# A linear-attention recurrence with two MLPs on one core: fewer, wider TensorE instructions and a later output part

## The chip, the cores and the metric

One core of a Trainium2 chip. The engines are TensorE (PE, with its weight loads PEld), VectorE (DVE), ScalarE (ACT), GpSimd (POOL) and SyncE (SP, which issues the DMAs). The metric is the device time of one execution in microseconds (us).

## The reference

A recurrence over 768 time steps for 4 x 8 heads with a 40 x 40 state each, then two MLPs over the 3072 x 320 result.

```python
for t in range(S):
    y[:, :, t] = np.einsum('bhd,bhde->bhe', rt, state)
    Sa = np.einsum('bhde,bhe->bhd', state, at)
    state = state * wt[:, :, None, :] - np.einsum('bhd,bhe->bhde', Sa, bt) + np.einsum('bhd,bhe->bhde', vt, kt)
h = x @ w_in;  solu = h * softmax(h);  x = layernorm(solu) * g_ln @ w_out    # first MLP, 320 -> 1024 -> 320
h = x @ w_in2; x = (max(h, 0) + alpha * min(h, 0)) @ w_out2                # second MLP, 320 -> 2048 -> 320
```

The weights arrive as 64-bit floats and are decoded to fp32 on the chip.

## The kernel before, in words

The 768 steps are 12 windows of 64 steps, each of two chunks of 32: 24 chunks, g = 0 to 23. The 32 heads lie in two halves e (partitions 0 to 63 and 64 to 127), each as 2 x 8 (pe, p). Within a chunk the recurrence is written as matrix products.

One call of slot (L1108) records chunk g. Its stages in order: load_g (L577) issues the loads of the next chunk's v (VUS, time-major; VUF, feature-major) and r (YS). stage_x (L591) multiplies a by state and v into px, copied to XP. stage_u (L607) multiplies by the chunk's inverse NT into pu, copied to VUS as U. stage_uf (L630) makes U again, feature-major, in pf, copied to VUF. stage_i (L645) puts the state into the bank pst with an identity matmul, stage_st (L658) adds the products of k and b with v and U there, and ACT copies the new state to the other VUS buffer. stage_g2 (L696) makes the masked products of r with k and U (pg, then DVE times mask into YS). stage_s (L681) brings the new state to the layout of KBS (pss). stage_y (L718) makes the output py, which DVE scales to Yt and ACT and DVE split into high and low parts Y. After an odd chunk x_move (L748) stores Y to DRAM (xd) and loads it back as xt, the first MLP's input.

Between these stages side (called at the points a to z of a slot) records gen1 (L454, chunk products of a with k and b), trans (L556, kbf transposed into KBS) and the two matmul parts of the inverse for four chunks (units, L526), whose other steps run on DVE.

The first MLP is cut into tasks (mlp_tasks, L1058): in slot g the queue gets mm1 of token tile g - 3 (16 matmuls h), the transposes tr1 and the 8 matmuls mm2 (po, with weights wo) of tile g - 4, and tr2 (ptx). They stand in one queue, in order, and are put where the recurrence would wait.

PE, ACT, DVE and POOL have their order written out by a planner that runs while the program is built: now[0] is its clock, note (L239) adds a duration, run books the other engines, until (L308) goes on when a value is due and pops tasks (pop, L273) or, where none is ready, zero or busy matmuls; pace (L293) notes a group of matmuls and fills in where too few array columns were counted lately. The transfers' order on SP is left to the framework. bank gives one of 4 PSUM banks. On the chip each engine takes its own list in order and waits for semaphores.

The first four slots have no MLP tasks but the last of them; their fillers are busy matmuls (L326), later ones zero (L286). The last four token tiles of the first MLP run after the slots, interleaved with the second MLP (phase2).

Of the kernel before, what the change touches and what calls it, by code (L numbers as in the profile page):

```python
# [27 lines left out]
KQ, RES = 8, 10  # L28
# [16 lines left out]
def tile_kernel(ctx: ExitStack, tc: tile.TileContext, w_fm, a0_fm, a_fm, kb_fm, r_fm, v_fm, v_tm,  # L45
# [117 lines left out]
    queue, now, seen = [], [0.0], []  # L163
# [333 lines left out]
    def inverse(W):  # L497
# [28 lines left out]
        def units(p, lhsT, rhs, rows, ls):  # L526
            for l in ls:
# [28 lines left out]
    def trans(w, q):  # L556
# [49 lines left out]
    def stage_u(g):  # L606
# [4 lines left out]
        for p in range(8):  # L611
# [12 lines left out]
    def blank(p):  # L624
# [3 lines left out]
        note(0.11 * p.shape[1] / 8, 8 * p.shape[1])  # L628

    def stage_uf(g, pe):  # L630
        NT, l0 = st["NT", g // 4], (g % 4) * 8
        vuf = VUF[g % 2]
        pf, bk = bank([128, 8, 32], "pf")
        blank(pf)
        for p in range(8):
            for e, o in EO:
                q = 2 * e + pe
                r = slice(q * 32, q * 32 + 32)
                nc.tensor.matmul(pf[o:o + 40, p, :], lhsT=XP[r, p * D:p * D + D], rhs=NT[r, l0 + p, :],  # L639
                                 start=True, stop=True)  # L640
            pace(0.08, 32)
        t = run("A", 0.38, lambda: nc.scalar.copy(out=vuf[:, pe * 8:pe * 8 + 8, 1, :], in_=pf[0:104]), now[0] + PL)
# [996 lines left out]
```

## Time and profile before

| | us |
|---|---|
| median of 3 timed runs (lowest, highest) | 1143.43 (1137.14, 1145.4) |
| the profiled execution: its own time | 1150.15 |
| its span, first to last instruction | 1148.4 |
| PE busy in the span | 1049.8 |
| the slots | about 72 to 747 |

Up to 38 us the first windows are prepared. The first chunk's stage_x runs there; it then waits for the first inverse. From 72 us on the slots follow one another until the last py at 746 us; then come the rest of the first MLP and the second, where PE is busy nearly throughout.

### The profile page before, as it was taken

The page shows a single profiled execution, that of the slowest core. Times are in us where ns is not written, and L with a number is a line of the kernel's source. Part 1 is how long each engine was busy: PE and PEld are TensorE (multiplying, and loading weights), DVE is VectorE, ACT ScalarE, POOL GpSimd, SP SyncE. Part 2 cuts the span into 40 slices and gives each one's busy share as a digit, 9 for nine tenths or more (in the row PEclk, how much of TensorE's full clock was granted, in tenths as well). Part 3 has the DMA queues.
Part 4 walks back from the last instruction along what each step waited for, and adds up shares of the span by engine and source line. Part 5 has one row for each costly group of instructions (what it writes and reads, how often), then busy time and mean ns, then how long its engine had stood idle before and what let it go on. Part 6 is the DMA issues. An engine that isn't in the chain of part 4 may idle for free.

```text
span 1148.4 us, 42660 instructions
## 1 busy us (share of the span) xinstructions
PE 1049.8 (91%) x19078; PEld 818.5 (71%) x19078; DVE 615.7 (54%) x1150; ACT 553.0 (48%) x1269; POOL 298.6 (26%) x352
## 2 busy tenths in 40 slices
PE   6689788889989998989898899989999999999997
PEld 2456566566667666756676667778899999999997
DVE  8838576657587745864765132354444444444333
ACT  1446437565678556844755466668512121212121
POOL 7401020112221321132201110234333333333333
PEclk9689788899999898988998899999999999999998
DMA  6613334352545353433634232246302020201010
GB/s 172 183 47 100 96 85 119 107 152 57 155 127 140 93 151 86 106 93 94 173 82 128 80 93 63 70 158 187 126 1 69 1 69 1 69 1 46 1 24 14
DMA packets 103169, 103.95 MB, mean 91 GB/s; under 512 B 37828, under 2 KB 80580, under 8 KB 102980
## 3 DMA queue, kind: packets, MB, share of 16 engines
q1 hardware_dynamic: 102980, 101.16, 31.9%
q8 instruction: 151, 2.47, 0.9%
q14 instruction: 38, 0.31, 0.1%
HBM read 75.71 MB, written 25.43 MB: 88 GB/s over the span
## 4 chain that ended last, share of the span: by engine, by line
PE 75%; DMA 7%; issue 5%; ACT 5%; DVE 3%; POOL 1%; SPq 1%; POOLq 0%; DVEq 0%; ACTq 0%
PE ph L1274 15%; PE po L841 9%; PE h L771 7%; PE acc L1292 5%; PE acc L1293 5%; PE acc L1294 5%; PE pf L639 3%; PE pss L687 3%; PE py L728 3%; PE zero L286 2%; PE pst L667 2%; PE busy L326 2%; DMA raw<-in_w_in_dram 2%; PE pst L654 2%; PE pg L706 2%
## 5 line engine op out<-in xcount | busy, mean ns | idle before, releaser
L1281 POOL TENSOR_TENSOR gll<-gt,gh 128x512 fp32r<-128x512 f32 (+1 forms) x112 | 128.1, 1144 | 227.9 <-ACT gh L1280 226.9
L806 DVE TENSOR_SCALAR gt<-ph,al 128x512 f32<-128x512 f32 (+1 forms) x112 | 75.5, 675 | 201.7 <-PE ph L1274 201.5
L1280 ACT CAST gh<-gt 128x512 fp32r<-128x512 f32 (+1 forms) x112 | 62.4, 558 | 250.3 <-DVE gt L807 213.4
L841 PE MATMUL po<-wo,ln 128*128 128x320 f32 x384 | 133.1, 484 | 2.4 <-ACT ln L833 1.7
L841 PEld LDWEIGHTS po<-wo,ln 128*128 128x128 f32 x384 | 74.5, 207 | 30.6 <-issue 7.1
L771 PE MATMUL h<-w1h,xt 128*128 128x512 f32 x240 | 95.9, 455 | 0.0
L1292 PE MATMUL acc<-w2h,gh 128*128 128x320 f32 x288 | 88.8, 308 | 0.0
L1293 PE MATMUL acc<-w2l,gh 128*128 128x320 f32 x288 | 88.8, 308 | 0.0
L1294 PE MATMUL acc<-w2h,gll 128*128 128x320 f32 x288 | 88.7, 308 | 0.0
L583 POOL MEMSET YS<- 64x512 f32 x44 | 23.1, 524 | 228.7 <-PE py L728 227.5
L902 POOL TENSOR_TENSOR raw<-em 128x512 f32<-128x512 f32 (+1 forms) x28 | 42.6, 1527 | 122.4 <-DVE em L893 77.7
L713 DVE TENSOR_TENSOR YS<-pg,mask 64x256 f32<-64x256 f32 x96 | 40.5, 422 | 57.1 <-PE pg L706 55.5
L807 DVE SCALAR_TENSOR_TENSOR gt<-ph,gt 128x512 f32<-128x512 f32 (+1 forms) x112 | 68.8, 615 | 3.8
L771 PE MATMUL h<-w1l,xt 128*128 128x512 f32 x144 | 66.9, 465 | 0.6 <-issue 0.6
L1274 PE MATMUL ph<-w1h,w2h 128*128 128x512 f32 x180 | 59.3, 394 | 0.0
L786 POOL TENSOR_TENSOR sm<-sm,const 128x1 f32<-128x1 f32 x24 | 14.2, 590 | 165.0 <-ACT sm L783 165.0
L567 ACT COPY KBS<-pt 64x160 f32<-64x160 f32 x192 | 55.1, 287 | 3.1 <-PE pt L563 0.5
L1293 PEld LDWEIGHTS acc<-w2l,gh 128*128 128x128 f32 x288 | 54.1, 188 | 1.4
L1292 PEld LDWEIGHTS acc<-w2h,gh 128*128 128x128 f32 x288 | 54.1, 188 | 1.3
L1294 PEld LDWEIGHTS acc<-w2h,gll 128*128 128x128 f32 x288 | 54.1, 188 | 0.0
L771 PEld LDWEIGHTS h<-w1h,xt 128*128 128x128 f32 x240 | 47.9, 209 | 8.5
L881 DVE TENSOR_SCALAR em<-raw 128x512 int32<-128x512 int32 (+1 forms) x39 | 17.8, 456 | 67.1 <-DMA raw<-in_w_in_dram 46.2
(186 smaller groups left out, 2407.3 us busy)
## 6 DMA issues: line engine op xcount, KB each, us to landing
kbf<-in_kb_fm_dram SPq DMA_DIRECT2D x24, 416.0 KB
x2d<-x SPq DMA_DIRECT2D x24, 320.0 KB
raw<-in_w_in_dram SPq DMA_DIRECT2D x14, 512.0 KB
raw<-in_w_out_dram SPq DMA_DIRECT2D x13, 512.0 KB
xd<-Y SPq DMA_DIRECT2D x24, 256.0 KB
xt<-xd SPq DMA_DIRECT2D x12, 512.0 KB
wt<-in_w_fm_dram SPq DMA_DIRECT2D x24, 211.7 KB
VUS<-in_v_tm_dram SPq DMA_DIRECT2D x48, 80.0 KB
```

Source lines behind the costliest of these rows:

```text
L567: t = run("A", 0.29, lambda k=k, c=c, r=r, o=o: nc.scalar.copy(out=k[r:r + 64, 1 - r // 64, q * 4:q * 4 + 4, :], in_=pt[64 * c:64 * c + 64 ...
L771: nc.tensor.matmul(st["h"][:, ns], lhsT=l, rhs=r, start=j == 0, stop=j == len(ops) - 1)
L806: nc.vector.tensor_scalar(out=tmp, in0=h, scalar1=0.0, scalar2=al, op0=ALU.min, op1=ALU.mult)
L807: nc.vector.scalar_tensor_tensor(out=o, in0=h, scalar=0.0, in1=tmp, op0=ALU.max, op1=ALU.add)
L841: nc.tensor.matmul(po, lhsT=st["ln", t][:, piece], rhs=wo1[:, piece], start=piece == 0, stop=piece == K1 - 1)
L902: (nc.vector if eng == "V" else nc.gpsimd).tensor_tensor(out=o, in0=f32(m), in1=f32(e), op=ALU.mult)
L1274: nc.tensor.matmul(p, lhsT=l, rhs=r, start=j == 0, stop=j == len(ops) - 1)
L1280: nc.scalar.copy(out=gh, in_=t)
L1281: nc.gpsimd.tensor_tensor(out=gll, in0=t, in1=f32(gh), op=ALU.subtract)
L1292: nc.tensor.matmul(acc, lhsT=gh[:, cs], rhs=oh, start=f == 0, stop=False)
L1293: nc.tensor.matmul(acc, lhsT=gh[:, cs], rhs=ol, start=False, stop=False)
L1294: nc.tensor.matmul(acc, lhsT=gll[:, cs], rhs=oh, start=False, stop=f == K2 - 1)
```

## The change

It has seven parts. (1) gen1 and stage_g2 use one weight tile of 64 columns where they used two of 32. (2) stage_uf makes U feature-major with transposes of VUS rows, 16 to a bank of its own for each half e, in place of products of XP with NT. (3) stage_i is gone: stage_st starts its own bank, and DVE adds the old state while it writes the new one. (4) stage_s uses transposes, with a bank for each half. (5) uf, g2 and y of chunk g - 1 stand in slot g, the load of r and feature-major v after that y; the last slot holds the parts of both chunks. (6) the planner's note counts PE instructions into pages of 128 and lets its clock wait for a page; pace may pop tasks ahead of such a wait. (7) the points of trans move.

```diff
+PAGE, FETCH, RATE = 128, 3.7, 0.03
...
-KQ, RES = 8, 10
+KQ, RES, SPARE = 8, 10, 6
...
-    def note(dt, n):
+    def note(dt, n, r=0):
+        page[0] += r
+        if page[0] >= PAGE and not plain():
+            page[0] -= PAGE
+            t, page[1] = page[1] + FETCH, max(now[0], page[1] + FETCH)
+            while now[0] < t:
+                note(min(0.1, t - now[0]), 0)
...
+    def early():
+
+        return page[1] + FETCH - now[0] - (PAGE - page[0]) * RATE
...
-    def pace(dt, n):
-
-        note(dt, n)
+    def pace(dt, n, r, spare=False):
+
+        note(dt, n, r)
+        while spare and head() and len(queue) > SPARE and early() > 0.3:
+            pop()
...
             for pe in range(2):
...
+                nc.tensor.matmul(pg[64 * pe:64 * pe + 64, p], lhsT=kbf[:, pe * 8 + p, c].rearrange("p i t -> p (i t)"),
+                                 rhs=x[0:104, :, pe, p, :], start=True, stop=True)
+            pace(0.115, 256, 4, True)
...
-                pace(0.072, rows)
+                pace(0.072, rows, 8, True)
...
-            pace(0.1, 208)
+            pace(0.1, 208, 1, True)
...
-    def load_g(g):
+    def load_v(g):
         w, c = divmod(g, 2)
-        v, y = VUS[g % 2], YS[g % 2]
-        vuf = VUF[g % 2]
+        for e in range(2):
+            q = 64 * e
+            nc.sync.dma_start(out=VUS[g % 2][q:q + 32, e], in_=v_tm[w, c, e])
+        put(("v_in", g))(now[0] + 2 * DMA)
+
+    def load_r(g):
+        w, c = divmod(g, 2)
+        y, vuf = YS[g % 2], VUF[g % 2]
         if g > 1:
             for e in range(2):
                 run("P", 0.6, lambda e=e: nc.gpsimd.memset(y[64 * e:64 * e + 64, e], 0.0), now[0] + PL)
         for e, r0 in EO:
-            q = 64 * e
-            nc.sync.dma_start(out=v[q:q + 32, e], in_=v_tm[w, c, e])
             nc.sync.dma_start(out=y[r0:r0 + 40, e], in_=r_fm[w, c, e])
             nc.sync.dma_start(out=vuf[r0:r0 + 40, :, 0], in_=v_fm[w, c, e])
-        put(("v_in", g))(max(now[0], free["P"]) + 2 * DMA)
+        put(("r_in", g))(max(now[0], free["P"]) + 2 * DMA)
...
-    def stage_uf(g, pe):
-        NT, l0 = st["NT", g // 4], (g % 4) * 8
...
-    def stage_i(g):
-        v = VUS[g % 2]
+        note(0.11 * p.shape[1] / 8, 8 * p.shape[1], 1)
+
+    def stage_uf(g):
+        v, vuf = VUS[g % 2], VUF[g % 2]
         until(("U", g, 0), ("U", g, 1))
...
+        for e, o in EO:
+            q = slice(64 * e + 32, 64 * e + 64)
+            pf, bk = bank([128, 16, 32], "pf")
+            for s in range(16):
+                nc.tensor.transpose(pf[0:40, s, :], v[q, e, s, :], ident[q, q])
+                pace(0.045, 16, 1)
+            t = run("A", 0.62, lambda: nc.scalar.copy(out=vuf[o:o + 40, :, 1, :], in_=pf[0:40]), now[0] + PL)
+            ring[bk] = t + LAT
+            put(("uf", g, e))(t + LAT)
 
     def stage_st(g, pe):
         k, v, vn = KBS[g % 4], VUS[g % 2], VUS[(g + 1) % 2]
         until(("U", g, pe), ("kb", g))
-        p_, bk = st["ps", g][pe]
+        p_, bk = bank([128, 8, 40], "pst")
         for p in range(8):
             for e, o in EO:
                 q, s = slice(64 * e, 64 * e + 64), pe * 8 + p
-                nc.tensor.matmul(p_[o:o + 40, p, :], lhsT=k[q, 1 - e, s, :], rhs=v[q, e, s, :], start=False,
-                                 stop=p == 7, skip_group_check=True)
-            pace(0.08, 80)
+                nc.tensor.matmul(p_[o:o + 40, p, :], lhsT=k[q, 1 - e, s, :], rhs=v[q, e, s, :], start=True, stop=True)
+            pace(0.08, 80, 4)
         for e, o in EO:
             sl = slice(pe * 8, pe * 8 + 8)
             d = vn[o:o + 40, e, sl, :]
-            t = run("A", 0.43, lambda d=d, o=o: nc.scalar.copy(out=d, in_=p_[o:o + 40]), now[0] + PL)
+            t = run("V", 0.5, lambda d=d, o=o, e=e: nc.vector.tensor_tensor(
+                out=d, in0=p_[o:o + 40], in1=v[o:o + 40, e, sl, :], op=ALU.add), now[0] + PL)
             ring[bk] = t + LAT
             if g % 4 == 3:
                 rs = st[(g + 1) // 2]["rs"]
...
     def stage_s(g, pe):
         kn, vn = KBS[(g + 1) % 4], VUS[(g + 1) % 2]
         until(("vus", g + 1, pe))
-        p_, bk = bank([128, 8, 40], "pss")
...
         for e, o in EO:
-            t = run("A", 0.42, lambda e=e, o=o: nc.scalar.copy(
-                out=kn[o:o + 40, 1 - e, pe * 8:pe * 8 + 8, :], in_=p_[o:o + 40]), now[0] + PL)
-        ring[bk] = t + LAT
+            p_, bk = bank([128, 8, 40], "pss")
+            for p in range(8):
+                nc.tensor.transpose(p_[0:40, p, :], vn[o:o + 40, e, pe * 8 + p, :], ident[o:o + 40, o:o + 40])
+                pace(0.045, 40, 1)
+            t = run("A", 0.42, lambda e=e, o=o, p_=p_: nc.scalar.copy(
+                out=kn[o:o + 40, 1 - e, pe * 8:pe * 8 + 8, :], in_=p_[0:40]), now[0] + PL)
+            ring[bk] = t + LAT
         put(("ks", g + 1, pe))(t + LAT)
...
     def stage_g2(g, half):
         y, vuf = YS[g % 2], VUF[g % 2]
         if half == 0:
-            until(("uf", g, 0), ("uf", g, 1), ("v_in", g))
+            until(("uf", g, 0), ("uf", g, 1), ("r_in", g))
             st["pg2"] = bank([128, 8, 2, 32], "pg2")
         pg, bk = st["pg2"]
         for p in range(half * 4, half * 4 + 4):
             for pe in range(2):
...
+                s = pe * 8 + p
+                nc.tensor.matmul(pg[64 * pe:64 * pe + 64, p], lhsT=vuf[:, s].rearrange("p i t -> p (i t)"),
+                                 rhs=y[0:104, :, s, :], start=True, stop=True)
+            pace(0.115, 256, 4)
...
             for q in range(4):
-                turn(2 * W + 1, q, p(0, 'a'), p(1, 'b'))
+                turn(2 * W + 1, q, p(0, 'd'), p(1, 'b'))
             for q in range(4):
-                turn(2 * W + 2, q, p(2, 'a'), p(3, 'b'))
+                turn(2 * W + 2, q, p(2, 'd'), p(3, 'b'))
...
         if g + 1 < NG:
-            load_g(g + 1)
+            load_v(g + 1)
         stage_x(g)
         slot_tasks(g)
         side(g, "a")
+        if g:
+            stage_uf(g - 1)
         side(g, "b")
         if g == 0:
             st["busy"] = st["idle"]
...
             for f in st["joins"]:
                 f()
         stage_u(g)
-        stage_uf(g, 0)
-        stage_uf(g, 1)
+        if g:
+            stage_g2(g - 1, 0)
+            stage_g2(g - 1, 1)
         side(g, "c")
         due((nd + 3) // 4)
         if not fin:
-            stage_i(g)
             stage_st(g, 0)
             stage_st(g, 1)
-        stage_g2(g, 0)
+        side(g, "x")
         due((nd + 1) // 4)
         if g == NG - 2:
             early_w()
-        side(g, "x")
+        if g:
+            stage_y(g - 1)
+        if g + 1 < NG:
+            load_r(g + 1)
         side(g, "d")
-        stage_g2(g, 1)
-        side(g, "e")
         due((nd + 2) // 4)
         if not fin:
             stage_s(g, 0)
             stage_s(g, 1)
+        side(g, "e")
         due(nd // 4)
         side(g, "f")
         flush(RES)
-        stage_y(g)
         side(g, "z")
+        if fin:
+            stage_uf(g)
+            stage_g2(g, 0)
+            stage_g2(g, 1)
+            stage_y(g)
         flush(0 if fin else KQ)
```

In the MLP's task tuples and in the other calls of pace a number of instructions is added.

PE in slot 22, from stage_u on, before (pf is stage_uf, pst stage_i and stage_st, pg stage_g2, po a task of the MLP):

```order
L614 MATMUL pu<-XP,LMN_167 32x40 x32
L626 LDWEIGHTS D_150
L626 MATMUL pf<-D_150 32x256
L639 MATMUL pf<-LMN_167,XP 40x32 x16
L626 LDWEIGHTS D_150
L626 MATMUL pf<-D_150 32x256
L639 MATMUL pf<-LMN_167,XP 40x32 x14
L841 MATMUL po<-wo_148,ln 128x320 x5
L639 MATMUL pf<-LMN_167,XP 40x32 x2
L654 MATMUL pst<-VUS_170,ident 40x320 x4
L667 MATMUL pst<-VUS_170,KBS_160 40x40 x32
L706 MATMUL pg_12076<-YS_174,VUF_172 32x64 x32
```

and in the changed kernel, from stage_x on:

```order
L614 MATMUL px<-VUS_170,XS_156 32x40 x32
L652 MATMUL pf<-ident,VUS_171 40x32 x32
L629 MATMUL pu<-XP,LMN_167 32x40 x32
L837 MATMUL po<-wo_148,ln 128x320 x4
L701 MATMUL pg_11141<-YS_175,VUF_173 64x64 x16
L665 MATMUL pst<-VUS_170,KBS_160 40x40 x32
L837 MATMUL po<-wo_148,ln 128x320 x2
L641 LDWEIGHTS D_150
L641 MATMUL py<-D_150 32x512
L724 MATMUL py<-YS_175,KBS_159 40x32 x32
```

The blank and identity matmuls of pf and pst are gone, the count of pg is halved, and pf, pg and py belong to the chunk before and stand ahead of stage_u and on both sides of stage_st.

PE in slot 9, the place of the first matmuls h that read the xt of the window that ends with chunk 7, before:

```order
L599 MATMUL px<-VUS_171,XS_155 32x40 x32
L286 LDWEIGHTS D_150
L286 MATMUL zero<-D_150 128x512
L855 MATMUL ptx<-ident,xs 128x128 x2
L855 MATMUL ptx<-ident,xs 64x128
L771 MATMUL h<-w1h,xt 128x512
L614 MATMUL pu<-XP,LMN_168 32x40 x32
```

and in the changed kernel:

```order
L851 MATMUL ptx<-ident,xs 128x128 x2
L851 MATMUL ptx<-ident,xs 64x128
L297 LDWEIGHTS D_150
L297 MATMUL zero<-D_150 128x512
L701 MATMUL pg_5146<-YS_174,VUF_172 64x64 x16
L297 LDWEIGHTS D_150
L297 MATMUL zero<-D_150 128x512
L665 MATMUL pst<-VUS_171,KBS_159 40x40 x16
L767 MATMUL h<-w1h,xt 128x512
L665 MATMUL pst<-VUS_171,KBS_159 40x40 x16
```

Before, y of chunk 7 stands at the end of slot 7, a whole slot ahead of these rows, and the first h before stage_u. In the changed kernel y of chunk 7 is in slot 8, and the first h of slot 9 stands within stage_st.

The state's way in slot 9. On ACT before, with the copies from pst:

```order
L619 COPY VUS_170<-pu 32x320 x4
L642 COPY VUF_172<-pf 104x8x32
L885 ACTIVATE em<-em,const 128x256
L886 ACTIVATE em<-em 128x256
L642 COPY VUF_172<-pf 104x8x32
L833 COPY ln<-ptr 128x512 x2
L673 COPY VUS_171<-pst 40x320 x4
L791 ACTIVATE P,sm<-h,sm 128x1024
L479 ACTIVATE GR<-pg 32x8x32 x8
```

and on DVE in the changed kernel (em<-raw is the first step of decoding weights that a DMA brings, YS the mask of stage_g2, x the second part of tr2):

```order
L709 TENSOR_TENSOR YS_174<-pg_5146,mask 64x256 x4
L877 TENSOR_SCALAR em<-raw 128x256
L878 TENSOR_SCALAR em<-raw 128x256
L670 TENSOR_TENSOR VUS_170<-pst,VUS_171 40x320 x2
L856 TENSOR_TENSOR x_5140<-ptx,x_5140 128x2x128
L857 TENSOR_TENSOR x_5140<-ptx,x_5140 64x128
L670 TENSOR_TENSOR VUS_170<-pst,VUS_171 40x320 x2
```

The state left ACT's list for DVE's, where the additions stand behind a decoding step that needs a load.

## Rows read from the trace of the kernel before

**Rows 1.** The page: busy time of PE; the queue of instruction fetches.

```profile
PE 1049.8 (91%) x19078; PEld 818.5 (71%) x19078; DVE 615.7 (54%) x1150; ACT 553.0 (48%) x1269; POOL 298.6 (26%) x352
...
q8 instruction: 151, 2.47, 0.9%
```

**Rows 2.** Busy time by stretch (length, busy and count by engine, PEclk, DMA).

```profile
72.00:170.00 98.00, 84.64 (x2687) 58.32 (x2687) 66.72 (x134) 51.14 (x121) 12.57 (x22) 0.88 0.33 92
170.00:747.00 577.00, 526.03 (x13221) 381.12 (x13209) 331.04 (x663) 360.33 (x860) 110.07 (x152) 0.93 0.40 109
```

**Rows 3.** Waits of PE, 72 to 747 us: total us, times, longest us.

```profile
PE pv L529 <- issue: 8.4, 5, 3.5
PE pg L468 <- ACT VUS L673: 7.2, 2, 5.5
...
PE h L771 <- issue: 0.6, 1, 0.6
```

**Rows 4.** Busy time from 66 to 92 us, columns as in rows 2.

```profile
66.00:92.00 26.00, 22.83 (x921) 15.73 (x922) 14.16 (x26) 14.16 (x33) 1.69 (x3) 1.00 0.22 61
```

**Rows 5.** DMA queues from 66 to 92 us (packets, MB, share).

```profile
q8 instruction: 7, 0.11, 1.9%
```

**Rows 6.** Timeline of PE: start us, us, what, xcount [idle before].

```profile
73.70 0.28 PE L626 MATMUL pf<-D 104*32 104x256 bf16 x1
...
75.59 1.90 PE L326 MATMUL busy<-busy 128*128 128x512 bf16 x8
77.42 1.28 PE L654 MATMUL pst<-VUS,ident 104*40 104x320 f32 x8
78.63 1.42 PE L667 MATMUL pst<-VUS,KBS 64*40 64x40 f32 x64
...
80.45 2.22 PE L468 MATMUL pg<-XS,kbf 104*32 104x64 f32 x127
...
85.00 0.81 PE L687 MATMUL pss<-ident,VUS 40*40 40x40 f32 x32
85.74 1.47 PE L326 MATMUL busy<-busy 128*128 128x512 bf16 x6
...
88.73 1.42 PE L728 MATMUL py<-YS,KBS 104*40 104x32 f32 x64
90.08 0.80 PE L599 MATMUL px<-VUS,XS 104*32 104x40 f32 x64
...
106.23 1.65 PE L563 MATMUL pt<-ident,kbf 104*128 104x104 f32 x16
```

**Rows 7.** Groups of PE by shape: count, busy us, mean ns, idle.

```profile
L841 PE MATMUL po<-wo,ln 128*128 128x320 f32 x384 | 133.1, 484 | 2.4 <-ACT ln L833 1.7 <-DVE wo L899 0.7
...
L855 PE MATMUL ptx<-ident,xs 128*64 128x128 f32 x24 | 6.9, 288 | 0.0
```

**Rows 8.** Groups of ACT by shape, 72 to 747 us, as rows 7.

```profile
L673 ACT COPY VUS<-pst 40x320 f32<-40x320 f32 x92 | 38.7, 420 | 19.2 <-PE pst L667 17.6
...
L642 ACT COPY VUF<-pf 104x256 f32<-104x256 f32 x48 | 17.3, 372 | 26.9 <-PE pf L639 26.5
```

**Rows 9.** A group of DVE by shape, 72 to 747 us.

```profile
L860 DVE TENSOR_TENSOR x<-ptx,x 128x256 fp32r<-128x256 f32 x19 | 8.1, 424 | 40.0 <-ACT x L865 39.8
```

**Rows 10.** Timeline of SP's DMA issues, two stretches: start us, us, what.

```profile
475.14 2.82 SPq L755 DMA_DIRECT2D xd<-Y  x4
481.03 0.40 SPq L756 DMA_DIRECT2D xt<-xd  x1
...
598.97 2.88 SPq L755 DMA_DIRECT2D xd<-Y  x4
...
609.18 1.33 SPq L757 DMA_DIRECT2D xt<-xd  x1
```

**Rows 11.** Waits of DVE, 72 to 747 us: total us, times, longest us.

```profile
DVE em L881 <- DMA raw<-in_w_in_dram: 46.2, 8, 11.7
...
DVE em L881 <- DMA raw<-in_w_out_dram: 20.6, 6, 6.4
```

More of the change, by code (lines that the diff above doesn't have):

```diff
@@ L160, in tile_kernel @@
     EO = ((0, 64), (1, 0))
-    queue, now, seen = [], [0.0], []
+    queue, now, seen, page = [], [0.0], [], [0, 0.0]
     INF = 1e9
@@ L274, in pop @@
         if head():
-            dt, n, f, _ = queue.pop(0)
+            dt, n, f, _, r = queue.pop(0)
             f()
         elif "busy" in st:
-            dt, n = 0.216, 512
+            dt, n, r = 0.216, 512, 1
             keep(1)
         else:
-            dt, n = 0.216, 416
+            dt, n, r = 0.216, 416, 1
             if "z" not in st or len(ring) - st["z"][1] >= 4:
@@ L627, in blank @@
                          rhs=D1[:, 0:16 * p.shape[1]].bitcast(BF16), start=True, stop=True)
-        note(0.11 * p.shape[1] / 8, 8 * p.shape[1])
-    def stage_uf(g, pe):
-        NT, l0 = st["NT", g // 4], (g % 4) * 8
[L632 to L642, printed above, removed]
-        ring[bk] = t + LAT
-        put(("uf", g, pe))(t + LAT)
-    def stage_i(g):
-        v = VUS[g % 2]
-        until(("U", g, 0), ("U", g, 1))
-        st["ps", g] = []
-        for pe in range(2):
-            p_, bk = bank([128, 8, 40], "pst")
-            for e, o in EO:
-                nc.tensor.matmul(p_[o:o + 40], lhsT=ident[0:104 - 8 * e, o:o + 40],
-                                 rhs=v[0:104 - 8 * e, e, pe * 8:pe * 8 + 8, :],
-                                 start=True, stop=False, skip_group_check=True)
-                pace(0.28, 640)
-            st["ps", g].append((p_, bk))
+        note(0.11 * p.shape[1] / 8, 8 * p.shape[1], 1)
+    def stage_uf(g):
+        v, vuf = VUS[g % 2], VUF[g % 2]
+        until(("U", g, 0), ("U", g, 1))
+        for e, o in EO:
[7 more added lines that the diff above has]
+            put(("uf", g, e))(t + LAT)
     def stage_st(g, pe):
@@ L703, in stage_g2 @@
             for pe in range(2):
-                for i in range(2):
-                    o, s = 64 * pe + 32 * i, pe * 8 + p
-                    nc.tensor.matmul(pg[o:o + 32, p], lhsT=vuf[:, s, i, :], rhs=y[0:104, :, s, :], start=True, stop=True)
-            pace(0.115, 256)
+                s = pe * 8 + p
+                nc.tensor.matmul(pg[64 * pe:64 * pe + 64, p], lhsT=vuf[:, s].rearrange("p i t -> p (i t)"),
+                                 rhs=y[0:104, :, s, :], start=True, stop=True)
+            pace(0.115, 256, 4)
         if half == 0:
```

34 lines of the change are left out of this document (12 added, 22 removed).

## The prediction

> **What bounds the kernel now.** I read the page first: TensorE (PE) is busy for 1049.8 us of the span with 19078 matmuls, far ahead of every other engine [rows 1]. The table by stretches comes next. The recurrence's slots lie between 72 and 747 us, 98 + 577 = 675 us; in them PE is busy 84.64 + 526.03 us at a mean granted clock of 0.88 and 0.93, DVE only 66.72 + 331.04 = 398 us, ACT 51.14 + 360.33 = 411 us [rows 2]. The change touches nothing after 747 us but the last chunk's output, so the slots are where it is decided, and there it is PE that decides.
>
> Third, what PE waits for in the slots. The reader is to see two kinds of wait. In ten rows, of which the first and the last stand here (8.4 to 0.6 us, 41.7 us in sum), the releaser is "issue": no semaphore and no buffer held PE. In seven more (20.8 us in sum, the largest among them 7.2) it is named as ACT or DVE [rows 3]. The "issue" waits belong to the instruction stream: the page has 151 packets of 2.47 MB on the instruction queue, so 16.4 KB a packet and 19078 / 151 = 126 matmuls with their weight loads [rows 1]. I call 126 matmuls a page. From 66 to 92 us, where nearly all is small matmuls, the clock was granted in full (1.00), 921 matmuls ran and PE still stood idle for some 3 us [rows 4], and 7 pages came in those 26 us [rows 5]: 26 / 7 = 3.7 us a page. So a page that holds less than 3.7 us of array work makes PE wait.
>
> **The change part by part.** All rates are from bursts in that stretch at full clock, start to next start [rows 6]. The sum stands against the profiled execution's 1150.15 us; the median of the three timed runs is 6.7 us lower, and I carry the sum over to it unaltered.
>
> State carried by an identity matmul (stage_i): 8 instructions take 78.63 - 77.42 = 1.21 us a slot, 23 slots: -27.8 us. Nothing on PE replaces it; the addition goes to DVE (below).
>
> U feature-major (stage_uf): two blank matmuls and 64 small ones take 75.59 - 73.70 = 1.89 us a slot, 45.4 us in 24 slots. Now 32 transposes. That a transpose is one instruction where a plain fp32 matmul is two shows in the counts: 24 chunks give 24 transposes with 64 columns of weights, and 8 x 24 matmuls of wo give 384 instructions [rows 7]. The price of a 40-column transpose is in no row. Lower end: 16 transposes of 104 columns in 1.65 us are 103 ns each, scaled by the moved columns 32/104 = 32 ns. Upper end: the whole 103 ns. Nearest in shape is py, with the same 40 weight columns and 32 moved: 64 in 90.08 - 88.73 = 1.35 us, 21 ns each with two halves of the array side by side, so 42 ns for one half alone. Consecutive transposes of a bank use one half, so I take 42: 24 x 32 x 0.042 = 32.3 us, or -13.1 us (ends -20.8 and +33.7).
>
> State to KBS (stage_s): 64 instructions as two bursts of 85.74 - 85.00 = 0.74 us, 34.0 us in 23 slots, become 32 transposes: 30.9 us, -3.1 us (ends -4.6 with 40 ns, +41.8 with 103 ns).
>
> 64-column weights in gen1 and stage_g2: a burst of 127 instructions lasts 2.22 us, at most 17.5 ns each, 1.12 us for a chunk's 64. Scaling py's 42 ns by 64/40 gives 67 ns on one half, 34 ns with two halves, 1.08 us for 32. So nothing on the array: 0 us (were the wider loads twice that, +1.1 us for each of some 44 chunk parts, about +48; were they as cheap as now, -24).
>
> Fillers: the changed order holds 18 more zero and 38 more busy matmuls. Eight busy ones took 77.42 - 75.59 = 1.83 us, 0.23 each: +12.9 us.
>
> Pages: the four edits remove 48 + 184 + 768 + 736 + 1536 = 3272 instructions and the fillers add 56, 3216 fewer, 25 pages. I laid both orders into pages of 126 and priced each by the bursts' rates. Before, 72 of the slots' 132 pages hold less than 3.7 us of work and lack 83 us in all; after, 34 of 107 lack 32 us. The changed rules also put MLP matmuls into the small bursts, which is part of that drop. Of the 83 us that this gives before, the trace shows 41.7 as waits, half; so half of the 51 us saved: -26 us (ends: 41.7 x 38/72 = -22, and -51).
>
> Clock: 98 x 0.12 + 577 x 0.07 = 52 us of full-speed time are lost to stretches at the lower of the two levels (1.2 instead of 2.4 GHz) [rows 2]. Fewer waits may give some back, at most in the ratio of the waits removed, 26 of 62.5, which is -22. But in the nearest stretch with fetch waits throughout the clock was 1.00 [rows 4], so I take -6 (ends 0 and -22).
>
> Work that moves: ACT loses 92 state copies (38.7 us) and its 48 U copies (17.3 us) double from 256 to 512 elements, at most 34.6 us [rows 8], so ACT gets lighter by 21 us or more. DVE gains 92 additions of 320 elements; the nearest row is a subtraction from PSUM of 256 elements at 424 ns [rows 9], by size at most 424 x 320/256 = 530 ns, 49 us in all. DVE would be busy 398 + 49 = 447 of about 617 us: hidden under PE, 0 us; if that cover were gone, +49. In DVE's queue the masks, scans and softmax steps behind an addition wait for it. SP: the v load stays at the head of the slot; r and v_fm loads and two GpSimd memsets go behind the previous chunk's y, and the decode's raw loads are queued behind them. They are needed a slot later, so 0 us.
>
> Output a slot later: xt is now written mid-slot and wanted in the next slot. From the first store of Y to a load of xt 6 to 10 us pass (475.14 to the first at 481.03, 598.97 to the last at 609.18) [rows 10]; for the transfer behind it the 3 us from the last store's end (475.14 + 2.82) to 481.03 are a guide, and Yt and Y lie before it with some 2 us: an estimate of 11 to 16 us. Between y and the first h the changed order holds about 16 us of PE work at these rates. Mostly in time, at times late: 11 windows, +5 us (ends 0, +20).
>
> Sum: -27.8 - 13.1 - 3.1 + 0 + 12.9 - 26 - 6 + 5 = -58.1. 1150.15 becomes 1092.0, the median 1143.43 becomes **1085.3**.
>
> **Rivals.** (1) DVE takes over the wait. The state now passes through DVE, which stood 46.2 + 20.6 = 66.8 us in 14 waits for raw weights, up to 11.7 us [rows 11]; in the changed order a split of raw stands right ahead of such an addition. If all 14 reach PE in full in place of the 20.8 us that semaphores cost now, +46: 1131 us. Against it: the next slot's x is a third of a slot away.
>
> (2) xt is late in every window, the slower end. PE takes its queue in order, so the first h that finds no xt stops the recurrence behind it. The point is (58 + 5) / 11 = 5.7 us of lateness per window; from there on the gain is gone. With 8 us: 1085 - 5 + 88 = 1168 us. For it: [rows 10] show 10 us once before any transfer. Against it: 16 us of work lie between.
>
> (3) The small transposes do not run as one instruction: 1504 instructions and 12 pages come back and each transpose costs two passes, 1504 x 0.042 = 63 us, with some 4 us of page waits: 1152 us. Against it: the 64-column transposes count once [rows 7]. The Trainium skill, page "TensorEngine Tiling (Array Packing)", section "Restrictions and Gotchas", says that column tiling excludes transpose mode for fp32. By that rule the time would be rival 3's; the counted row disagrees for 64 columns, and no run yet shows 40 columns on 32 rows.
>
> **How the numbers follow.** Forecast 0.72, rival 1 0.16, rival 2 0.08, rival 3 0.04. About 1% is what a measurement tells from no change: below 1132 us is faster. The forecast's own spread is 1045 (page saving at its full 51 and part of the clock's 22) to about 1115 (transposes dearer by 20 ns, 30 us); rival 1 lies on the border, split 0.10 faster, 0.05 same, 0.01 slower. So faster 0.82, same 0.09, slower 0.09, and the range 1045 to 1130 leaves out rivals 2 and 3 and the far ends.
>
> **What would show it.** Right: instruction packets near 126 instead of 151; "issue" waits of PE in the slots near 20 us; transposes of pf and pss counted 768 and 736, about 42 ns start to start; no identity matmul; last y near 690 us. Wrong: PE waiting for DVE's addition or for xt by tens of us, bursts of transposes near 100 ns, or as many "issue" waits over fewer pages.

## The result and the profile after

The changed kernel takes 1111.09 us (median of 4 runs, 1100.35 to 1115.87) against 1143.33 us for the kernel before on the same chip: 0.971 of it, interval 0.963 to 0.980. It is faster, by 32 us where I had forecast 58. Ratios leave out runs more than 1.5% above the fastest of their kernel; e2's and e10's below, from two runs each, therefore lie under what their medians give, and the profiles of these two are of such slower runs.

The page of the changed kernel, the lines that answer to [rows 1]:

```profile
PE 1010.7 (91%) x15862; PEld 790.0 (71%) x15862; DVE 653.8 (59%) x1242; ACT 526.5 (47%) x1177; POOL 298.7 (27%) x352
...
q8 instruction: 126, 2.06, 0.8%
```

126 packets, as foretold, and still 126 matmuls to a packet. The stretches, columns as in [rows 2]. The last Yt is written at 715.4 us and Y stored from 717.7, before at 746.6 and 748.4; so 715.8 us stands here for the 747 of [rows 2]:

```profile
72.00:170.00 98.00, 87.40 (x2306) 57.49 (x2295) 74.98 (x150) 50.39 (x120) 14.21 (x20) 0.88 0.36 95
170.00:715.80 545.80, 492.05 (x10768) 361.11 (x10766) 365.49 (x740) 342.48 (x790) 110.01 (x154) 0.92 0.43 115
```

Subtract PE's busy time from the length: 643.8 - 579.45 = 64.35 us are left, and before 675.0 - 610.67 = 64.33 [rows 2]. So the whole gain of 31 us in this stretch is less busy time of PE. PE stands as long as it did, and I had forecast 26 us less of that. The part behind it is 5 us shorter as well (1112.4 - 715.8 = 396.6 us against 401.4).

The stretch hides a loss at its start: the first matmul of stage_u is at 80.2 us in the changed kernel, before at 71.9 (rows up to 200 us: the count, the shortest, median and longest time in ns, the first and last start):

```profile
L614 PE MATMUL pu<-XP,LMN x320: 191/197/271, 71.9 to 176.8; 32*32 32x40 f32 x160
...
L629 PE MATMUL pu<-XP,LMN x384: 197/197/219, 80.2 to 197.0; 32*32 32x40 f32 x192
```

So the slots proper got some 39 us shorter, and 8 us were lost ahead of them, which the forecast has no term for; why the first inverse comes later there wasn't tested.

What PE stands for has changed. Waits of PE from 72 to 715.8 us in the changed kernel, to be held against [rows 3]:

```profile
PE pst L665 <- ACT VUS L634: 9.4, 3, 8.7
PE pv L540 <- issue: 8.3, 4, 3.1
PE py L724 <- issue: 6.7, 4, 2.3
PE pss L685 <- DVE VUS L670: 6.2, 1, 6.2
PE py L724 <- DVE YS L709: 5.8, 2, 5.2
PE pf L652 <- ACT XP L617: 5.6, 1, 5.6
PE busy L339 <- issue: 3.5, 1, 3.5
```

All rows named "issue" sum to 25.7 us (41.7 before), those with a named releaser to 38.0 (22.5 before, in 12 rows from 7.2 down to 0.2). Four single stops of 8.7, 6.2, 5.6 and 5.2 us make two thirds of the latter. DVE's waits for raw weights, from 72 to 720 us, are as long as in [rows 11], 65.0 us:

```profile
DVE em L877 <- DMA raw<-in_w_out_dram: 50.5, 12, 12.1
...
DVE em L877 <- DMA raw<-in_w_in_dram: 14.5, 4, 8.4
```

The longest stop, followed back. Timelines of PE, ACT, DVE and SP in the changed kernel; the bracket holds the idle time ahead of a row and what ended it:

```profile
208.77 1.72 PE L665 MATMUL pst<-VUS,KBS 64*40 64x40 f32 x32 [8.66 <-ACT VUS L634]
...
207.04 0.72 ACT L881 ACTIVATE em<-em,const 128x512 int32<-128x512 int32 x1 [8.46 <-DVE em L877]
207.67 0.61 ACT L882 ACTIVATE em<-em 128x512 f32<-128x512 int32 x1
208.31 1.73 ACT L634 COPY VUS<-pu 32x320 f32<-32x320 f32 x4
...
206.58 0.43 DVE L877 TENSOR_SCALAR em<-raw 128x512 int32<-128x512 int32 x1 [12.14 <-DMA raw<-in_w_out_dram]
...
194.39 0.38 SPq L752 DMA_DIRECT2D xt<-xd  x1
194.87 0.42 SPq L362 DMA_DIRECT2D kbf<-in_kb_fm_dram  x1
195.39 0.34 SPq L753 DMA_DIRECT2D xt<-xd  x1
195.78 0.40 SPq L362 DMA_DIRECT2D kbf<-in_kb_fm_dram  x1
196.23 0.35 SPq L912 DMA_DIRECT2D raw<-in_w_out_dram  x1
196.63 0.79 SPq L373 DMA_DIRECT2D XS<-in_a_fm_dram  x2
```

Read it from below. SP issues a raw load right behind two loads of xt and two of kbf, and DVE can use it 10 us later. DVE's first decode step stands 12.14 us for it. ACT's decode step stands behind DVE's, and behind it in ACT's list are the copies of U that PE needs. The stop of 6.2 us ends in the same way, by the addition that the change put on DVE:

```profile
331.19 0.29 DVE L877 TENSOR_SCALAR em<-raw 128x256 int32<-128x256 int32 x1 [8.44 <-DMA raw<-in_w_in_dram]
331.40 0.29 DVE L878 TENSOR_SCALAR em<-raw 128x256 int32<-128x256 int32 x1
331.72 1.01 DVE L670 TENSOR_TENSOR VUS<-pst,VUS 40x320 f32<-40x320 f32 x2
...
332.27 1.30 PE L685 MATMUL pss<-ident,VUS 40*40 40x40 f32 x16 [6.20 <-DVE VUS L670]
```

The 5.6 us have ACT's copy of XP behind a decode step (DVE had stood 7.70 us for raw); the 5.2 us have DVE standing 7.41 us for a load of XS. The Trainium skill, page "PSUM — Partial Sum Buffer", section "Engine vs sequencer instructions", says that the queues of ScalarE, VectorE and GpSimdE are strictly first in, first out. These rows agree with that: ACT's list stood for 8.46 us behind one step.

And such a stop costs more than its length. Busy time around the longest, with the granted clock as the third number from the end:

```profile
192.00:200.00 8.00, 7.77 (x144) 4.58 (x140) 2.39 (x3) 6.36 (x17) 0.84 (x2) 1.00 0.63 164
200.00:208.80 8.80, 0.14 (x2) 0.03 (x1) 2.19 (x5) 1.71 (x4) 0.00 (x0) 0.76 0.61 147
204.60:221.70 17.10, 12.40 (x173) 8.16 (x174) 13.67 (x27) 6.93 (x14) 2.74 (x4) 0.50 0.30 76
221.70:230.00 8.30, 7.78 (x97) 5.68 (x98) 6.11 (x13) 3.26 (x8) 0.00 (x0) 1.00 0.22 67
```

At the full level PE ran without a break up to 200 us, then it stood; for 17.1 us, 12.9 of them after it resumed, the clock was at the lower level, 1.2 GHz. The stops of 6.2, 5.6 and 5.2 us go with 10, 6.8 and 13.7 us at 0.50 (331 to 341, 368.4 to 375.2, 450.3 to 464). Over the whole stretch 98 x 0.12 + 545.8 x 0.08 = 55 us of full-speed time are lost to the lower level, as before (52). The stretches at the four stops hold 47.6 us at half the clock, so 24 of the 55 us.

### The profile page after: what moved, and what is told of

Its sections match the earlier page's. It is cut to its first block, busy times and chain, and to the rows that moved or that the text cites. A ratio compares the mean times of both kernels' runs of the same rounds, so it can differ in the third digit from the quotient of the medians.

```text
span 1112.4 us, 36263 instructions
## 1 busy us (share of the span) xinstructions
PE 1010.7 (91%) x15862; PEld 790.0 (71%) x15862; DVE 653.8 (59%) x1242; ACT 526.5 (47%) x1177; POOL 298.7 (27%) x352
## 4 chain that ended last, share of the span: by engine, by line
PE 68%; DMA 9%; DVE 9%; ACT 6%; issue 5%; POOL 2%; SPq 1%; DVEq 0%; POOLq 0%; ACTq 0%
PE ph L1279 15%; PE po L837 8%; PE h L767 6%; PE acc L1299 5%; PE acc L1297 5%; PE acc L1298 5%; DMA raw<-in_w_out_dram 3%; PE busy L339 3%; PE py L724 3%; PE zero L297 2%; PE pst L665 2%; PE pf L652 2%; PE pg L701 2%; PE pss L685 2%; DMA kbf<-in_kb_fm_dram 2%
## 5 line engine op out<-in xcount | busy, mean ns | idle before, releaser
L837 PEld LDWEIGHTS po<-wo,ln 128*128 128x128 f32 x384 | 71.7, 201 | 26.4 <-issue 4.5
L898 POOL TENSOR_TENSOR raw<-em 128x512 f32<-128x512 f32 (+1 forms) x28 | 38.0, 1364 | 128.8 <-issue 64.2
L339 PE MATMUL busy<-busy 128*128 128x512 bf16 x212 | 65.3, 462 | 6.7 <-issue 3.5
L372 POOL MEMSET XS<- 32x512 f32 (+1 forms) x36 | 18.7, 520 | 150.8 <-PE px L614 149.8
L687 ACT COPY KBS<-pss 40x320 f32<-40x320 f32 x92 | 38.4, 417 | 37.3 <-PE pss L685 35.5
L490 ACT ACTIVATE GR<-pg 32x256 f32<-32x256 f32 x96 | 36.1, 376 | 41.0 <-PE pg L479 39.8
L709 DVE TENSOR_TENSOR YS<-pg,mask 64x256 f32<-64x256 f32 x96 | 40.4, 421 | 24.5 <-PE pg L701 22.6
L877 DVE TENSOR_SCALAR em<-raw 128x512 int32<-128x512 int32 (+1 forms) x39 | 16.3, 419 | 65.2 <-DMA raw<-in_w_out_dram 50.5
```

The lines of the kernel that those rows point to most:

```text
L339: nc.tensor.matmul(st["busy"], lhsT=busy[:, 0:128], rhs=busy, start=True, stop=True)
L837: nc.tensor.matmul(po, lhsT=st["ln", t][:, piece], rhs=wo1[:, piece], start=piece == 0, stop=piece == K1 - 1)
```

## The experiments

All twelve together first. The time is the median of a kernel's runs, the ratio is to the kernel before on the same chip. "Raw" is DVE's standing at raw loads; "issue" and "named" are PE's waits in the profiled run, all from 72 us to the last store of Y; "lost" is that length times one minus its granted clock, by the two stretches up to and from 170 us. In the profiles of e1 to e8 about 20 matmuls of fillers have no record (their weight loads have one), so up to some 5 us of their "issue" were work.

| kernel | us | ratio | raw | issue | named | lost |
|---|---|---|---|---|---|---|
| before | 1143.3 | 1 | 66.8 | 41.7 | 22.5 | 52 |
| changed | 1111.1 | 0.971 [0.963, 0.980] | 65.0 | 25.7 | 38.6 | 55 |
| e1 state on ACT | 1094.9 | 0.956 [0.952, 0.960] | 34.0 | 16.3 | 23.4 | 47 |
| e2 raw later | 1104.3 | 0.957 [0.950, 0.964] | 10.2 | 31.0 | 18.0 | |
| e3 no page model | 1158.6 | 1.014 [1.009, 1.019] | 102.7 | 31.6 | 64.4 | 60 |
| e4 output not later | 1144.7 | 1.000 [0.996, 1.003] | 34.6 | 37.2 | 32.6 | 54 |
| e5 = e3 + raw later | 1102.7 | 0.963 [0.958, 0.968] | 17.8 | 33.7 | 19.4 | 39 |
| e6 = e1 + raw later | 1104.7 | 0.967 [0.962, 0.972] | 29.3 | 16.0 | 28.2 | 37 |
| e7 before, raw later | 1129.9 | 0.988 [0.984, 0.992] | 8.3 | 48.8 | 7.0 | 33 |
| e8 before + part 6 | 1129.3 | 0.984 [0.975, 0.993] | 36.0 | 35.0 | 9.4 | 27 |
| e9 = e8 + parts 5, 7 | 1162.3 | 1.015 [1.009, 1.021] | 25.8 | 28.3 | 22.2 | 50 |
| e10 = e1 less part 1 | 1138.8 | 0.987 [0.980, 0.995] | | | | |
| e11 loads on GpSimd | 1143.0 | 0.998 [0.994, 1.003] | 73.1 | 23.2 | 65.5 | 67 |
| e12 = e1 + e11's move | 1134.7 | 0.993 [0.989, 0.997] | 39.9 | 14.4 | 49.2 | 63 |

On the whole the last two columns go together: where PE waits 7 to 9 us for others, 27 to 33 us are lost to the lower level, where it waits 49 to 66, 60 to 67.

**e1, part 3 undone.** stage_i, the accumulating stage_st and ACT's copies are again as before, and the rest is the changed kernel.

```diff
+            stage_i(g)
...
-                nc.tensor.matmul(p_[o:o + 40, p, :], lhsT=k[q, 1 - e, s, :], rhs=v[q, e, s, :], start=True, stop=True)
+                nc.tensor.matmul(p_[o:o + 40, p, :], lhsT=k[q, 1 - e, s, :], rhs=v[q, e, s, :], start=False,
+                                 stop=p == 7, skip_group_check=True)
...
-            t = run("V", 0.5, lambda d=d, o=o, e=e: nc.vector.tensor_tensor(
-                out=d, in0=p_[o:o + 40], in1=v[o:o + 40, e, sl, :], op=ALU.add), now[0] + PL)
+            t = run("A", 0.43, lambda d=d, o=o: nc.scalar.copy(out=d, in_=p_[o:o + 40]), now[0] + PL)
```

> The changed kernel with its third part undone: the state is carried by identity matmuls again and copied by ACT, DVE no longer adds it. In PE's order the fillers fall from 372 to 263 (zero matmuls from 160 to 50), the identity matmuls come back (184 instructions, 1.21 us a slot, 27.8 us). Theory DVE (the gain came out smaller because DVE, which takes its list in order and stands waiting for raw weights, now carries the state): the 28 us of identity matmuls are paid by the 109 fillers at 0.23 us (25 us) and by shorter waits of PE for DVE, so not slower than the changed kernel: 1085 to 1112 us, PE's waits named after ACT or DVE near the 21 us of before instead of 36. Rival PE (array time decides, fillers are free): 1111 + 28 = 1139 us.

1094.9 us: the work that the change took off PE, put back, saves 16 us. It beats both kernels. The groups of fillers in the changed kernel:

```profile
L339 PE MATMUL busy<-busy 128*128 128x512 bf16 x212 | 65.3, 462 | 6.7 <-issue 3.5 <-DVE busy L1192 1.8 <-POOL busy L1162 1.3
...
L297 PE MATMUL zero<-D 104*128 104x512 bf16 x160 | 44.6, 411 | 0.6 <-ACT KBS L578 0.6
```

and in e1:

```profile
L339 PE MATMUL busy<-busy 128*128 128x512 bf16 x193 | 54.8, 432 | 7.4 <-issue 3.8 <-DVE busy L1207 2.3 <-POOL busy L1177 1.3
...
L297 PE MATMUL zero<-D 104*128 104x512 bf16 x50 | 15.5, 437 | 1.4 <-ACT XP L617 0.9 <-ACT KBS L578 0.4
```

With the identity matmuls back, 109 fillers go, from 372 to 263: of the 213 busy matmuls whose weight loads stand in e1's profile, 20 have no record, so the 39.6 us by which these rows fall are about 35. And PE's waits fall by at least 24.6 us. So most of the 28 us of stage_i had been filled up again in the changed kernel's order; that the planner put the fillers there by its own rules and for what it expects of DVE is argued, not shown.

**e2, the planner expects raw loads later.** The estimate of a raw load's landing is 8.0 us in place of 3.5; only where decode steps stand in the order changes.

```diff
-            lane["next"].append((lane["tasks"].pop(0)(), now[0] + DMA))
+            lane["next"].append((lane["tasks"].pop(0)(), now[0] + LAND))
```

> The changed kernel with one number altered: the planner takes a load of raw weights to land 8 us after its issue instead of 3.5, so the first step of decoding stands later in DVE's list. Theory DVE: DVE's waits for raw fall from 65 us to under 35, PE's four long waits behind them (8.7, 6.2, 5.6 and 5.2 us) go or shrink to a sum under 12, against some 31 more fillers (7 us): 1090 to 1105 us. Rival (these waits of DVE are slack that PE would spend anyway): 1111 to 1120 us.

1104.3 us, in the range; the ratio of 0.957 meets the changed kernel's interval only at its edge. DVE's standing at raw goes from 65.0 to 10.2 us and PE's named waits from 38.6 to 18.0, with the state still on DVE. e5 below shows the same (17.8 and 19.4). With the stop followed above, this says that it is the late loads that reach PE, by way of DVE's and ACT's lists.

**e3, no page model, and e5, the same with raw later.**

```diff
-PAGE, FETCH, RATE = 128, 3.7, 0.03
+PAGE, FETCH, RATE = 1 << 30, 3.7, 0.03
...
-        while spare and head() and len(queue) > SPARE and early() > 0.3:
+        while False and spare:
```

> The changed kernel with its sixth part undone: the planner no longer counts pages, and no MLP task is popped ahead of a page. The instructions are the same but for 48 more fillers. Theory pages (the shorter instruction stream alone brings what it can, the model only orders it): issue waits of PE in the slots 28 to 40 us, time within 10 us of the changed kernel, 1105 to 1122. Rival (the model and the tasks moved into the small bursts carry the gain): issue waits back above 42 us and 1125 to 1140 us.

e3 is slower than the kernel before, beyond what either theory gave it, and not by fetches: its issue waits are 31.6 us, 6 more than with the model. Its named waits are 64.4, and DVE stands 102.7 us at raw:

```profile
DVE em L877 <- DMA raw<-in_w_in_dram: 76.0, 9, 14.4
...
DVE em L877 <- DMA raw<-in_w_out_dram: 26.7, 7, 8.3
```

> The changed kernel without the page model and the popped tasks (as in e3_no_page_model), and with the planner's estimate of a raw load's landing raised from 3.5 to 8.0 us (as in e2_raw_later). In e3 DVE stood 102.7 us at raw weights in the slots (65.0 in the changed kernel). Theory: what e3 loses is that the planner's clock runs ahead of the chip's, so that the decode steps are put where their raw weights have not landed, and DVE's additions of the state stand behind them; then the later estimate gives most of it back: DVE's waits at raw under 40 us, 1110 to 1130 us. Rival: the loss of e3 is in PE's own stream (pages of too little array work, MLP tasks out of place); then the waits at raw fall, but the time stays at 1145 to 1165 us.

1102.7 us, 56 us less than e3 by that one estimate, and below the theory's range. Beside e2 (0.957 with the model, 0.963 without, the intervals overlap) the page model is then worth nothing that can be told. So in the changed kernel the model's 4% came with the raw loads: 65.0 us of standing at them with it, 102.7 without. That it earned them by holding back the planner's clock, and with it the decode steps, is argued from its rules. The pages themselves are a small part: 6 and 3 us of issue waits in the two pairs.

**e4, the output not later.** Parts 5 and 7 undone: uf, g2 and y stand in the slot of their own chunk.

```diff
-        if g:
-            stage_uf(g - 1)
...
+        stage_uf(g)
...
-        if g:
-            stage_y(g - 1)
...
+        stage_y(g)
```

> The changed kernel with its fifth and seventh parts undone: uf, g2 and y of a chunk stand in its own slot again, with the loads at the slot's head and trans at its old points. Fillers rise from 372 to 471 (99 x 0.23 = 23 us). Theory slack (the later output lets PE work where it would wait): 1125 to 1145 us. Rival (the later output only costs, by the chunk of xt that comes late): 1095 to 1110 us.

1144.7 us, at the upper end of the theory's range and the time before: without the shift the changed instructions gain nothing.

**e6, both mends.** e1 and e2 together.

> Both mends at once: the state carried by the identity matmul and ACT's copies as before the change (e1_state_on_act, 1094.9 us), and the later estimate of the raw loads (e2_raw_later, 1104.3 us). Theory of one cause: both take away the same thing, PE standing behind DVE standing at raw weights; then the second adds little to the first: 1088 to 1100 us. Rival of two causes: raw loads also hold PE by another way than the state (the decoded weights of the MLP, the scans), and the gains add up: 1070 to 1086 us.

1104.7 us: nothing is added, even some 1% is lost against e1, outside both ranges but on the side of one cause. The later estimate, useful where DVE carries the state, had little left to take away here (raw 34.0 to 29.3 us).

**e7 and e8, the kernel before with one thing.** e7 has the later raw estimate; e8 has part 6, with its own counts (8, 4 or 2 instructions for a step).

> The kernel before with the estimate of the raw loads' landing raised to 8.0 us and nothing else. Its DVE stood 66.8 us at raw weights, about as long as the changed kernel's, but no state passed through DVE. Theory: that standing was off PE's path there, and the time stays within 1% of the kernel before: 1133 to 1150 us, with DVE's waits at raw under 30 us. Rival: standing at raw cost PE as much before, so this gains as in the changed kernel or more: 1105 to 1130 us.

> The kernel before with part 6 alone: the page model and the popped tasks, counted with its own instructions (8 for a pair of rows of gen1 and g2, 2 for an identity matmul). Theory, after e3: the model carries much of the gain by itself, since small bursts get MLP matmuls beside them: 1105 to 1128 us, with fewer issue waits of PE in the slots than the 41.7 us before. Rival: the model is worth something only once there are fewer instructions, since with 151 pages the fetch can't be kept up with whatever stands in them: 1135 to 1155 us.

1129.9 and 1129.3 us. e7 is at the edge of the rival's range: standing at raw had cost the kernel before 1.2%, if less than the 5% that it makes between e3 and e5. e8 lies at the upper edge of its theory's range. Its issue waits fall only from 41.7 to 35.0; the named ones fall to 9.4 and the time lost to the lower level from 52 to 27 us. DVE's standing at raw falls too, to 36.0 us, so what of its gain is the pages' isn't separated from the raw loads':

```profile
72.00:170.00 98.00, 88.24 (x2751) 59.94 (x2766) 75.48 (x158) 57.06 (x131) 11.88 (x22) 0.95 0.40 110
170.00:722.60 552.60, 518.14 (x13251) 369.47 (x13247) 312.66 (x630) 353.08 (x848) 102.79 (x152) 0.96 0.40 109
```

**e9, the kernel before with parts 5 to 7**, and **e10, e1 with 32-column weights.**

```diff
-                nc.tensor.matmul(pg[64 * pe:64 * pe + 64, p], lhsT=vuf[:, s].rearrange("p i t -> p (i t)"),
-                                 rhs=y[0:104, :, s, :], start=True, stop=True)
+                for i in range(2):
+                    o, s = 64 * pe + 32 * i, pe * 8 + p
+                    nc.tensor.matmul(pg[o:o + 32, p], lhsT=vuf[:, s, i, :], rhs=y[0:104, :, s, :], start=True, stop=True)
```

> The kernel before with parts 5, 6 and 7 (the output a slot later, the page model, and the turns' new places), and with none of the instruction edits of parts 1 to 4. Theory: the shift's 33 us (e4 against the changed kernel) come from its own, whatever the instructions, so it goes as far below e8_before_pages (1129.3 us): 1090 to 1106 us, and the instruction edits together are worth nothing or less beside the changed kernel's 1111. Rival: the shift only repairs what the edits make late (U through 32 transposes and ACT's two wide copies before the output part can start), and is worth nothing without them: 1120 to 1135 us.

> e1_state_on_act (1094.9 us) with part 1 undone: four matmuls with 32-column weights again in place of two with 64, in gen1 and stage_g2. Theory (the term of nothing on the array): the array time is the same, and the 1536 instructions more, 12 pages, cost a part of their fetch: 1098 to 1115 us. Rival: the wide weights cost array time that the saved pages only make up for: 1080 to 1094 us.

Both fell out of every range, on the slow side. With the instructions before, the shift costs 3.1% (0.984 to 1.015); with the changed ones it gains 2.9% (e4 to the changed kernel). e9's rows:

```profile
72.00:170.00 98.00, 86.52 (x2419) 56.31 (x2419) 69.22 (x144) 55.03 (x134) 10.31 (x18) 0.91 0.41 114
170.00:762.50 592.50, 553.36 (x13632) 391.04 (x13631) 324.37 (x651) 361.56 (x864) 106.36 (x156) 0.93 0.38 103
```

Against e8, PE's idle time is only 6 us longer, its busy time 33.5 us (10 and 30 if e8's unrecorded fillers are counted as work); the lower level takes 23 us more of it, and 35 more fillers (349 against 314) some 8 at 0.23 us. Why the shift brings PE's clock down there isn't settled. The runs that differ by whole parts make a chain, each kernel with one step more: before 1; part 6 (e8) 0.984; parts 5 and 7 (e9) 1.015; the transposes, parts 2 and 4 (e10) 0.987; 64-column weights, part 1 (e1) 0.956; the state on DVE, part 3 (changed) 0.971. On another path the steps would have other sizes, as the shift's shows. Between e10 and e1 the order itself changes too: e10 holds 33 more fillers (296 against 263), some 8 us.

**e11 and e12, load_r's loads issued by GpSimd.** The v_fm loads go in two halves.

```diff
-            nc.sync.dma_start(out=y[r0:r0 + 40, e], in_=r_fm[w, c, e])
+            nc.gpsimd.dma_start(out=y[r0:r0 + 40, e], in_=r_fm[w, c, e])
```

> The changed kernel with the r and v_fm loads of load_r issued by GpSimd, where their memsets are, and not by SP (the v_fm loads in two halves). Theory: in SP's queue raw loads stand behind these loads, which wait for the last chunk's y (58.7 + 26.4 us of SP's waits in the slots); without them DVE's waits at raw fall from 65 us to under 45, and PE's stops behind DVE with them: 1092 to 1106 us. Rival: raw is late by the planner's estimate of 3.5 us, whatever stands ahead of it, and GpSimd's queue now stands for y ahead of its own raw work: 1108 to 1125 us.

> e1_state_on_act (1094.9 us) with the same move of load_r's loads to GpSimd. Theory: with the state on ACT, DVE's standing at raw reaches PE only through the output's py and the MLP, so the move gives little: 1085 to 1097 us. Rival: GpSimd's queue, which stores the decoded weights as well, becomes late: 1100 to 1115 us.

The theory fell, for both, and 1143.0 and 1134.7 us lie above the rivals' ranges as well. DVE stands at raw for 73.1 us in e11, and its second longest wait is the longest of the changed kernel, in the same place, with xt and kbf in front of the raw load on SP and nothing of load_r (last row: busy time by stretch):

```profile
189.58 0.38 SPq L753 DMA_DIRECT2D xt<-xd  x1
190.06 0.42 SPq L362 DMA_DIRECT2D kbf<-in_kb_fm_dram  x1
190.58 0.34 SPq L754 DMA_DIRECT2D xt<-xd  x1
190.97 0.40 SPq L362 DMA_DIRECT2D kbf<-in_kb_fm_dram  x1
191.42 0.35 SPq L913 DMA_DIRECT2D raw<-in_w_out_dram  x1
...
202.54 0.43 DVE L878 TENSOR_SCALAR em<-raw 128x512 int32<-128x512 int32 x1 [12.45 <-DMA raw<-in_w_out_dram]
...
191.00:202.00 11.00, 4.77 (x109) 2.65 (x106) 0.00 (x0) 3.13 (x7) 1.76 (x3) 0.81 0.80 201
```

The load takes 11 us from issue to use. It is 512 KB; ahead of it stand 512 and 128 KB of xt and twice 416 KB of kbf. These 1984 KB at the 201 GB/s of 191 to 202 us are an estimate of 10 us. So here the wait fits what else had been issued, with nothing of load_r in it. The rival's part came true beside it: GpSimd is busy with the issues themselves (group by line in e11):

```profile
L604 POOL DMA_DIRECT2D VUF<-in_v_fm_dram x96 | 71.0, 740 | 191.7 <-issue 173.8 <-DVE tmp L523 6.8 <-ACT sm L775 4.9
...
L602 POOL DMA_DIRECT2D YS<-in_r_fm_dram x48 | 29.6, 617 | 0.0
```

How much of the 32 us that e11 loses against the changed kernel is due to these 100 us on GpSimd isn't shown.

## Why the prediction was right, and where not

Sign and range were right; the gain was 32 us of 58. The range held because it was wide: what the forecast said of PE's waits, 21 us of the 58, did not come. By the steps:

- **Instructions and pages' number:** right. 126 packets; pf x768 and pss x736; no identity matmul.
- **Transposes** (-13.1 and -3.1): mis-sized, to the good. In the changed kernel's timeline of PE

```profile
188.09 0.95 PE L685 MATMUL pss<-ident,VUS 40*40 40x40 f32 x32
188.97 1.34 PE L837 MATMUL po<-wo,ln 128*128 128x320 f32 x4
...
342.51 1.01 PE L652 MATMUL pf<-ident,VUS 32*40 32x32 f32 x32
343.45 0.79 PE L629 MATMUL pu<-XP,LMN 32*32 32x40 f32 x64
...
443.55 1.15 PE L701 MATMUL pg<-YS,VUF 104*64 104x64 f32 x32
444.63 1.42 PE L665 MATMUL pst<-VUS,KBS 64*40 64x40 f32 x64
```

  32 transposes take 0.94 us (29 ns each) and 0.88 us (28 ns), not 42 ns: 24 x 0.94 = 22.6 us and 23 x 0.88 = 20.2 us at full clock, -22.8 and -13.8 if all ran so. By the tiles' busy time, 72 to 747 and 72 to 715.8 us, pf went from 54.4 to 28.0 us (-26.4), but pss only from 40.0 to 35.8 (-4.2): few of its 32 transposes stand in one piece, most come in eights and sixteens, at times at the lower clock (the 16 at 332.27 us took 1.30 us). So the term of pf was too small by half, and that of pss came out near only because two errors, in the rate and in how the transposes stand, cancel: that is luck. My nearest row, py with half its rate, was the wrong one; the lower end, a transpose scaled by its columns, was nearly right for pf. Rival 3 is out: each counts once and is short. The Trainium skill, page "TensorEngine Tiling (Array Packing)", section "Restrictions and Gotchas", says that column tiling excludes transposes of fp32. No row shows whether that case is met here; the time that rival 3 took from it did not come.
- **64-column weights** (0): right on the array, 444.63 - 443.55 = 1.08 us for 32, as worked out. That their 1536 instructions would count for more than that, 3.1% between e10 and e1, was not foreseen; by my pages' term they were worth 12 of 25 pages, 12 us, and some 8 us more are the fillers by which the two orders differ.
- **Fillers** (+12.9): 56 more, as counted, but 65.3 + 44.6 against 51.6 + 38.5 us before in the same groups, +19.8 or 0.35 us each and not 0.23.
- **Pages** (-26): the step that failed first. Issue waits went from 41.7 to 25.7 us, -16, not to near 20. And e3 with e5 shows that the model's gain came another way, with the raw loads. The Trainium skill, page "Runtime: NRT & Kernel Launch", section "Instruction fetch mechanics", calls the cost of crossing into the next block mostly hidden. Here PE stood 14 to 49 us in the table's "issue", so as far as these waits are fetches it was not.
- **ACT and DVE move, 0 with the cover:** the step that failed most. DVE's time was indeed hidden, its waiting was not: named waits of PE rose by 15.5 us (22.5 to 38.0; the prediction's 20.8 leaves out five rows of 0.5 us and less). Rival 1 had the mechanism and gave it all 46 us more; about a third came. It is wider than rival 1 said: two of the four long stops pass through ACT's list and not through the addition. With fillers this undid stage_i's -27.8: in e1 stage_i is back and the time is 1.5% lower.
- **Clock** (-6): 52 and 55 us lost, nothing came back; 24 of the 55 us stand at the four long stops.
- **xt late** (+5) and rival 2: no wait of PE for xt stands in the changed kernel's list. Right that it would be in time; too careful by 5 us.

In sum: the forecast's terms for PE's busy time make -27.8 - 13.1 - 3.1 + 12.9 - 6 = -37.1, measured are 579.45 - 610.67 = -31.2. By tile, pst went from 63.3 to 37.0 us, pf from 54.4 to 28.0, pss from 40.0 to 35.8, pg from 52.6 to 49.0 and the fillers from 60.5 to 78.5, together -42. Against that stand 4.6 us more of py, and 8.0 us of pn and pt, matmuls of the inverse and transposes of kbf that before ran ahead of 72 us. (Tiles overlap in time, so this doesn't add up to the last us.) The waits' terms, -26 + 5 = -21, came to 0. With the 4.8 us by which the part behind got shorter, the profiled time fell by 36.0 us and not by 58.1: 5.9 + 21 - 4.8 is that gap.

Open stay why the shift's sign depends on the instructions, what in e10 costs more than its 12 pages and 33 fillers (together some 20 of 35 us), and why the changed kernel's first slot begins 8 us late.

## What to carry to other kernels

An engine at 60% that stands for a load isn't free: look what is behind the waiting instruction in its list before you move work of the critical path there, and add the waits of the engine to its busy time. In an order planned ahead, a wrong landing estimate can be worth as much as an instruction edit: one constant moved these kernels by 1 to 5%, once the wrong way (e6). And work taken from an engine that is kept busy with fillers on purpose may only be replaced by fillers; count them in the new order before the saving is booked.

## What was not expected of the hardware

- Each of the changed kernel's four stops of PE of 5 to 9 us went with 7 to 17 us at the lower clock level, which began before the stop ended, so that it cost more than its length.
- Transposes with 40 weight columns run at 28 to 29 ns start to start where 32 stand together, below the 42 ns of one half of py's rate.
- A 512 KB load issued behind four others of 1472 KB in sum was usable only 10 to 11 us after its issue, in the same place of two kernels.
- The order alone moves much: e8 and e9 hold nearly the same instructions (19076 and 19111 by their weight loads) and are 3.1% apart; 23 of the 40 us between their slots are lost at PE's granted clock (0.96 and 0.93 from 170 us on).
